# Weight conversion in a three-layer float32 kernel: two 512-column pieces at a time, in 1024-column instructions

## The chip, the cores and the metric

The kernel runs on one core of one Trainium2 chip. The metric is the device time of one execution in microseconds (us), lower is better. Before the change three runs gave 1316.76, 1318.71 and 1318.84 us; the median is 1318.71.

The engines are named as the profile names them: PE is TensorE's matmul unit and PEld its weight load, DVE is VectorE, ACT is ScalarE, POOL is GpSimd, SP is SyncE, whose queue issues the DMAs here.

## What is computed

Cut from the reference (B, H, S, Ns, D = 8, 8, 512, 32, 64; d_model 512, d_ff 2048):

```python
scores = scale * np.matmul(x, state.transpose(0, 1, 3, 2))
a = softmax(scores)                      # over the 32 states
xread = np.matmul(a, state)
a2 = softmax(scale * np.matmul(state, x.transpose(0, 1, 3, 2)))
sread = np.matmul(a2, x)
x = np.concatenate([xread, sread], axis=2)   # 8 x 544 rows of 512
x = square(relu(x @ w_in)) @ w_out       # the kernel's w1, v1
x = elu(x @ w_in2) @ w_out2              # the kernel's w2, v2
```

The four weight matrices arrive as float64 and everything else as float32. A float32 product is made of three PE passes: each operand is split into a high and a low part of the type float32r, and hi*lo, hi*hi and lo*hi are summed.

## The kernel before

**Stages.** The work on 8 batches of 544 rows has three parts. In the first, batches 0 to 3 go singly through attention and the first layer (16 steps of f, one for 128 of the 2048 hidden columns); batches 4 to 7 go in pairs by an algorithm of seven products. In the second part the rows of state go through the first layer. In the third the second layer runs, again by seven products. The change touches the weights, which are converted while batches 0 to 3 are worked on; three pairs of v2 follow with the last pair of batches.

**Weights.** A piece is 128 rows by 512 columns of float64, so 512 KB. `load64` (line 210) issues its load on SP as 1024 int32 a partition, into the next of RAW = 5 raw tiles of 4 KB. `convert` (line 218) makes float32 of it: on ACT a Prelu that scales the high words (line 228), then a copy that turns the low words into an integer part (line 230); on DVE a clamp (232), a shift by three bits (233), and the addition of the low part (235). Each of the five instructions is 512 columns wide.

**What the four kinds of piece become.** w1's 16 pieces go by twos into eight tiles that stay (`conv_w1`, line 237). v1's 16 pieces are stored to DRAM (`d_v`), and split at once into high and low part, on ACT (line 254) and on DVE (line 256) (`conv_v1`, line 247). w2 and v2 are made in pairs j and j + 8 by `conv_pair` (line 283), stored, and summed and split for the seven products (`wf`, `f_w`, `f_v`).

**The order.** The list `pieces` holds four pieces of w1, then v1 and w1 by turns. `next_conv` moves every conversion that is under way on by one step, and starts the next if the `cv` tiles (CV = 4, of 2 KB) allow it; it is called four times after the scores of batch 0, four times after the operand of batch 0, and twice in each of its steps f. `next_load` issues one more load once a piece's raw tile has been read. A scheduler in the framework then fixes the order of the instructions of each engine; buffers and order decide every wait. Engines take their queue in order, and so does SP.

**Batch 0 at the start.** The scores (`sc`, line 349) are made, then m = w1 x state for a quarter of the hidden columns (`emit_m`: `mp` in bursts of eight 32-column matmuls, copied by ACT, lines 362 and 364, with the matrix `minus` between them); four such quarters m_0 to m_3 serve the 16 steps. A step f makes `h` from m (6 matmuls, lines 170 to 172), then on ACT `r` = relu (487), `g` and `gs` = squares (489, 491), on DVE the low part of gs (492), and two steps later 12 matmuls into `acc` with v1's f. While PE would wait in the first 25 us, `busy_pe` (line 530) lets it multiply `ident` with itself (`idle`, line 534).

Of the kernel before, what the change touches and what calls it, by code (L numbers as in the profile page):

```python
# [11 lines left out]
I32 = mybir.dt.int32  # L12
# [15 lines left out]
LAG = 2  # L28
RAW, WF, CV = 5, 3, 4
NF = 7  # L30
# [80 lines left out]
def attn_mlp_kernel(ctx: ExitStack, tc: tile.TileContext, xt, xn, st, w1, v1, w2, v2, outx, outs):  # L111
# [46 lines left out]
    gap(pool, "gap3", 48)  # L158
    wo_p = pool("wo", FC)
    gs_p = pool("gs", 3)  # L160
# [20 lines left out]
    if True:  # L181
        ident = const.tile([P, P], F32, name="ident")
        make_identity(nc, ident)
        minus = const.tile([P, P], F32R, name="minus")
        nc.scalar.activation(out=minus, in_=ident, func=AF.Copy, scale=-1.0)
# [23 lines left out]

        def load64(name, i):  # L210

            t = turn("raw", [P, 512, 2], I32, f"raw_{name}{i}")
            nc.sync.dma_start(out=t.rearrange("p f w -> p (f w)"), in_=src64[name][i].bitcast(I32))
            raw[name, i] = t

        pace, gate = [], []

        def convert(name, i, out):

            t = raw.pop((name, i))
            low, high = t[:, :, 0], t[:, :, 1]
            bits = out.bitcast(I32)
            after = pace if name in ("w2", "v2") else gate
            with tc.issue_after(after[0].ins) if after else nullcontext():
                nc.scalar.activation(out=out, in_=high.bitcast(F32), func=AF.Prelu, scale=2.0 ** -112, alpha=NEGATIVE)
            with tc.issue_after(gate[0].ins) if gate else nullcontext():
                nc.scalar.activation(out=low, in_=low.bitcast(U32), func=AF.Copy, scale=2.0 ** -29)  # L230
            yield
            nc.vector.tensor_scalar(out=out, in0=out, scalar1=CLAMP, scalar2=-NEGATIVE * CLAMP, op0=ALU.min, op1=ALU.max)
            nc.vector.tensor_single_scalar(out=bits, in_=bits, scalar=3, op=ALU.logical_shift_left)
            yield
            nc.vector.tensor_tensor(out=bits, in0=bits, in1=low, op=ALU.add)
# [11 lines left out]
        def conv_v1(f):  # L247
            v = conv_p["cv"].tile([P, 512], F32, name="cv", tag="cv")
            yield from convert("v1", f, v)
            next_load()  # L250
            d = wd["v1", f] = dram.tile([P, 512], F32, name=f"d_v1{f}", tag=f"d_v1{f}")
            nc.sync.dma_start(out=d, in_=v)
            t = wo_p.tile([P, 2, DM], F32R, name=f"v1_{f}", tag="wo")
            nc.scalar.activation(out=t[:, HI], in_=v, func=AF.Copy)
            yield
            nc.vector.tensor_tensor(out=t[:, LO], in0=v, in1=t[:, HI].bitcast(F32), op=ALU.subtract)
            wo_t["v1", f] = t

# [24 lines left out]
        def conv_pair(name, j):  # L283


            v = [conv_p["cv"].tile([P, 512], F32, name="cv", tag="cv") for _ in range(2)]
            for _ in zip_longest(convert(name, j, v[0]), convert(name, j + HF, v[1])):
                yield
            next_load()
            next_load()  # L290
            d = wd[name, j] = dram.tile([P, 2, 512], F32, name=f"d_{name}{j}", tag=f"d_{name}{j}")
            for r in range(2):
                nc.sync.dma_start(out=d[:, r], in_=v[r])
            for t in sums(v):
                yield
            w = wf[name, j] = dram.tile([P, NF, 2, 256], F32, name=f"f_{name}{j}", tag=f"f_{name}{j}")
            yield from put_split(w, ((1, v[0][:, :256].unsqueeze(1)), (2, v[1].rearrange("p (q f) -> p q f", q=2)),
                                     (2, t[:, :2]), (2, t[:, 2:])))

        def sums_v1(j):  # L300

            v = [conv_p["cv"].tile([P, 512], F32, name="cv", tag="cv") for _ in range(2)]
            for r in range(2):
# [17 lines left out]
        of_pairs = lambda pairs: [(name, r * HF + j) for name, j in pairs for r in range(2)]  # L321
        loading, busy = pieces + of_pairs(pairs2[:IN_SINGLE]), []
        pairs2 = pairs2[IN_SINGLE:]

        def next_load():
            if loading:
                load64(*loading.pop(0))

        def next_conv(more=True):

            for c, name in list(busy):
                if next(c, busy) is not None:
                    busy.remove((c, name))
            held = sum({"w1": 0, "v1": 1}.get(n, 2) for _, n in busy)
            if more and converting and (converting[0][0] == "w1" or held + (converting[0][0] != "v1") < depth["cv"]):
# [87 lines left out]
        def at_sread(b):  # L423
# [103 lines left out]
        for _ in range(RAW):  # L527
            next_load()

# [10 lines left out]
        gate.append(A[0]["exp"])  # L540
        for _ in range(KC):
            next_conv()
# [4 lines left out]
        at_soft2(0)  # L547
        for _ in range(4):
            next_conv(False)
# [10 lines left out]
        gate.append(copies[0])  # L560
        for _ in range(4):
            next_conv()
        gate.clear()
        later = {}
        for b in range(SINGLE):
# [124 lines left out]
        converting.extend(pairs2)  # L690
        loading.extend(of_pairs(pairs2))
        for _ in range(2):
            next_load()
        products, left = iter(()), 0
# [398 lines left out]
```

## Time and profile before

| | |
|---|---|
| runs, median | 1318.71 us (1316.76 to 1318.84) |
| profiled execution, first to last instruction (span) | 1314.0 us |
| profiled execution, own time | among the runs' values, 2.8 to 4.8 us above its span |
| PE busy | 1302.9 us, 7020 matmuls on record |
| DVE busy | 952.7 us, 1431 instructions |
| ACT busy | 845.4 us, 1429 instructions |
| DMA | 305.40 MB, mean 232 GB/s |

The profile is one execution taken by the hardware profiler. A row of the order of time names the start, the duration, the engine, the line, the operation, the tiles written and read, their shape, and how many equal instructions were merged; in brackets stand the idle time of the engine ahead of it and what ended that. A float32 matmul with 32 columns counts as two, and some matmuls lack a record. The duration of an instruction overlaps with the next one's, so what an instruction takes of its engine is the distance from its start to the next start. One add of integers (line 235) is counted in 16-bit halves, so its 512 columns read as 1024.

### The profile page before, as it was taken

How to read it: one execution, taken by the hardware profiler on the slowest of the kernel's cores; microseconds unless marked ns; L12 is line 12 of the kernel's file. 1: busy time of each engine (PE TensorE's matmuls, PEld its weight loads, DVE VectorE, ACT ScalarE, POOL GpSimd, SP SyncE). 2: the span in 40 equal slices, each digit the busy share in tenths (PEclk: the TensorE clock that was granted, in tenths of full speed). 3: DMA queues.
4: the chain of work that ended last, by engine and by line, in shares of the span. 5: the costliest groups of instructions: out<-in, count | busy, mean ns of one | idle time of the engine just before them, and what ended most of it. 6: DMA issues, size and time to landing. Idle time of an engine off the chain costs nothing.

```text
span 1314.0 us, 19733 instructions
## 1 busy us (share of the span) xinstructions
PE 1302.9 (99%) x7020; PEld 1042.5 (79%) x7020; DVE 952.7 (73%) x1431; ACT 845.4 (64%) x1429; POOL 0.7 (0%) x6
## 2 busy tenths in 40 slices
PE   8999999999999999999999999999999999999999
PEld 6677777777677777778988888888888888888888
DVE  6997878687869955895766963789546984568644
ACT  5997777787765667665567744675446743666444
POOL 0000000000000000000000000000000000000000
PEclk9999999999999999999999999999999999999999
DMA  7999987886734663589697678767786777778733
GB/s 264 321 326 360 336 310 255 294 299 241 266 107 140 203 196 112 166 285 316 207 316 193 196 210 256 237 192 210 215 282 191 209 208 230 204 207 288 220 115 113
DMA packets 138865, 305.40 MB, mean 232 GB/s; under 512 B 14736, under 2 KB 29072, under 8 KB 135696
## 3 DMA queue, kind: packets, MB, share of 16 engines
q1 hardware_dynamic: 138768, 304.15, 72.0%
q8 instruction: 56, 0.92, 0.3%
q14 instruction: 41, 0.34, 0.1%
HBM read 227.54 MB, written 76.55 MB: 231 GB/s over the span
## 4 chain that ended last, share of the span: by engine, by line
PE 83%; DVE 5%; ACT 3%; DMA 3%; issue 1%; SPq 0%; ACTq 0%; DVEq 0%
PE x L44 18%; PE X L44 13%; PE z L44 9%; PE Z L44 6%; PE acc L170 4%; PE acc L172 4%; PE acc L171 4%; PE h L170 4%; PE h L172 4%; PE h L171 4%; PE y L44 3%; PE Y L44 3%; PE mp L349 2%; PE as L44 2%; PE hs L44 1%; DVE g L82 1%
## 5 line engine op out<-in xcount | busy, mean ns | idle before, releaser
L176 DVE TENSOR_TENSOR gp<-g,gp 128x512 fp32r<-128x512 f32 (+1 forms) x224 | 212.4, 955 | 110.9 <-ACT gp L175 109.9
L175 ACT ACTIVATE gp<-g 128x512 fp32r<-128x512 f32 (+1 forms) x224 | 187.4, 843 | 149.8 <-PE x L44 73.8
L44 PE MATMUL x<-gp,wr 128*128 128x512 f32 x1152 | 273.6, 391 | 1.2 <-DVE gp L176 1.1
L44 PEld LDWEIGHTS x<-gp,wr 128*128 128x128 f32 x1152 | 214.8, 188 | 52.9 <-DVE gp L176 4.1
L44 PE MATMUL X<-xf,wr 128*128 128x512 f32 x768 | 186.9, 390 | 0.1
L44 PEld LDWEIGHTS X<-xf,wr 128*128 128x128 f32 x768 | 143.4, 188 | 32.1 <-ACT u L879 1.7
L44 PE MATMUL z<-gp,wr 128*128 128x512 f32 x576 | 133.5, 390 | 0.0
L44 PEld LDWEIGHTS z<-gp,wr 128*128 128x128 f32 x576 | 108.0, 188 | 23.5 <-issue 0.8
L875 DVE SCALAR_TENSOR_TENSOR g<-r,g 128x512 f32<-128x512 f32 x96 | 63.9, 689 | 64.7 <-ACT r L874 64.6
L170 PE MATMUL acc<-gs,v 128*128 128x512 f32 x256 | 103.1, 403 | 0.1
L170 PE MATMUL h<-at,m 128*128 128x512 f32 x256 | 101.6, 397 | 0.8 <-ACT m L175 0.5
L172 PE MATMUL acc<-gs,v 128*128 128x512 f32 x256 | 100.3, 392 | 0.0
L171 PE MATMUL acc<-gs,v 128*128 128x512 f32 x256 | 100.0, 391 | 0.0
L171 PE MATMUL h<-at,m 128*128 128x512 f32 x256 | 99.9, 390 | 0.0
L172 PE MATMUL h<-at,m 128*128 128x512 f32 x256 | 99.9, 391 | 0.0
L44 PE MATMUL Z<-xf,wr 128*128 128x512 f32 x384 | 97.4, 389 | 0.0
L873 ACT ACTIVATE r<-g 128x512 f32<-128x512 f32 x96 | 57.5, 625 | 59.6 <-DVE g L923 42.8
L82 DVE TENSOR_TENSOR g<-g,g 128x1024 f32<-128x1024 f32 x72 | 87.5, 1221 | 0.7
L44 PEld LDWEIGHTS Z<-xf,wr 128*128 128x128 f32 x384 | 72.1, 188 | 15.0
L874 ACT ACTIVATE r<-r 128x512 f32<-128x512 f32 x136 | 81.5, 621 | 0.7
L170 PEld LDWEIGHTS acc<-gs,v 128*128 128x128 f32 x256 | 48.0, 188 | 26.6 <-issue 9.2
L44 PE MATMUL y<-gp,wr 128*128 128x512 f32 x288 | 68.6, 389 | 0.0
(148 smaller groups left out, 2039.4 us busy)
## 6 DMA issues: line engine op xcount, KB each, us to landing
wr<-f_v SPq DMA_DIRECT2D x288, 256.0 KB, 3.1
wr<-f_w SPq DMA_DIRECT2D x224, 256.0 KB, 3.0
f_v<-wf SPq DMA_DIRECT2D x40, 512.0 KB, 4.0
raw_w<-in_w_dram SPq DMA_DIRECT2D x32, 512.0 KB, 5.2
raw_v<-in_v_dram SPq DMA_DIRECT2D x32, 512.0 KB, 5.5
f_w<-wf SPq DMA_DIRECT2D x24, 512.0 KB, 3.7
wr<-p_v SPq DMA_DIRECT2D x48, 256.0 KB, 3.9
xt<-in_xt_dram SPq DMA_DIRECT2D x8, 1024.0 KB, 6.6
```

Source lines behind the costliest of these rows:

```text
L44: nc.tensor.matmul(ps, wk[a], xk[b], start=start and k == 0 and i == 0, stop=last and k == len(w) - 1 and i == 2, skip_group_check=True)
L82: return lambda jj: tt(out=out[jj], in0=a[jj], in1=b[jj], op=ALU.subtract)
L170: mm(ps, w[HI], x[LO], start=first, stop=False)
L171: mm(ps, w[HI], x[HI], start=False, stop=False)
L172: mm(ps, w[LO], x[HI], start=False, stop=last)
L175: copy = nc.scalar.activation(out=hi, in_=src, func=AF.Copy)
L176: nc.vector.tensor_tensor(out=lo, in0=src, in1=hi.bitcast(F32), op=ALU.subtract)
L349: mm(ps[e][32 * k:32 * k + 32, :], st_t[b][r, k, :], x(k, r), start=True, stop=True)
L873: act(out=r, in_=h, func=AF.Relu, scale=-1.0)
L874: act(out=r, in_=r, func=AF.Exp, scale=-1.0)
L875: nc.vector.scalar_tensor_tensor(out=out, in0=r, scalar=-1.0, in1=h, op0=ALU.add, op1=ALU.max)
```

## The change

Raw tiles hold two pieces (8 KB, three of them), each half filled by a load of its own (`load64` has the half, r, as an argument). A pair is pieces 2i and 2i + 1 for w1 and v1, and j and j + 8 for w2 and v2. `convert` is 1024 columns wide in all its five instructions, and the split of v1 too; v1 and the pairs are stored by one DMA each. Three raw tiles of two pieces take the place of five of one, and two `cv` tiles of 4 KB that of four of 2 KB; with batches 6 and 7 it is one of each. To make room `minus` is put into the tile of the sums (`tf`) and `srs` into that of the exponentials (`t`). `next_pair` issues two loads. `next_conv` is called half as often to start something, and as often to go on.

```diff
-RAW, WF, CV = 5, 3, 4
+RAW, WF, CV = 3, 3, 2
...
-    wo_p = pool("wo", FC)
+    wo_p = pool("wo", FC // 2)
...
-        minus = const.tile([P, P], F32R, name="minus")
+        minus = conv_p["tf"].tile([P, P], F32R, name="minus", tag="tf")
...
-        def load64(name, i):
-
-            t = turn("raw", [P, 512, 2], I32, f"raw_{name}{i}")
-            nc.sync.dma_start(out=t.rearrange("p f w -> p (f w)"), in_=src64[name][i].bitcast(I32))
-            raw[name, i] = t
+        def load64(name, i, r):
+
+            if r == 0:
+                raw[name, i] = turn("raw", [P, 2, 512, 2], I32, f"raw_{name}{i}")
+            n = i + r * HF if name in ("w2", "v2") else 2 * i + r
+            nc.sync.dma_start(out=raw[name, i][:, r].rearrange("p f w -> p (f w)"), in_=src64[name][n].bitcast(I32))
...
-            low, high = t[:, :, 0], t[:, :, 1]
+            low, high = t[..., 0], t[..., 1]
...
         def conv_w1(i):
-            g, k = divmod(i, KC)
-            if k % 2 == 0:
-                half[g, k // 2] = wi_p.tile([P, 2, 512], F32, name=f"w1_{g}{k // 2}", tag="wi")
-            t = half[g, k // 2]
-            yield from convert("w1", i, t[:, k % 2])
-            next_load()
-            if k % 2:
-                w1_t[g, k // 2] = t
...
+            t = wi_p.tile([P, 2, 512], F32, name=f"w1_{i}", tag="wi")
+            half[i // 2, i % 2] = t
+            yield from convert("w1", i, t)
+            next_pair()
+            w1_t[i // 2, i % 2] = t
...
+        def conv_v1(i):
+            v = conv_p["cv"].tile([P, 2, 512], F32, name="cv", tag="cv")
+            yield from convert("v1", i, v)
+            next_pair()
+            d = dram.tile([P, 2, 512], F32, name=f"d_v1{i}", tag=f"d_v1{i}")
             nc.sync.dma_start(out=d, in_=v)
...
+            t = wo_p.tile([P, 2, 2, DM], F32R, name=f"v1_{i}", tag="wo")
+            nc.scalar.activation(out=t[:, :, HI], in_=v, func=AF.Copy)
+            yield
+            nc.vector.tensor_tensor(out=t[:, :, LO], in0=v, in1=t[:, :, HI].bitcast(F32), op=ALU.subtract)
...
-            v = [conv_p["cv"].tile([P, 512], F32, name="cv", tag="cv") for _ in range(2)]
-            for _ in zip_longest(convert(name, j, v[0]), convert(name, j + HF, v[1])):
-                yield
-            next_load()
-            next_load()
+            v = conv_p["cv"].tile([P, 2, 512], F32, name="cv", tag="cv")
+            yield from convert(name, j, v)
+            next_pair()
...
-            for r in range(2):
-                nc.sync.dma_start(out=d[:, r], in_=v[r])
+            nc.sync.dma_start(out=d, in_=v)
+            v = (v[:, 0], v[:, 1])
...
-        pieces = [("w1", i) for i in range(4)]
-        for i in range(16):
-            pieces += [("v1", i)] + ([("w1", i + 4)] if i < 12 else [])
+        pieces = [("w1", i) for i in range(2)]
+        for i in range(8):
+            pieces += [("v1", i)] + ([("w1", i + 2)] if i < 6 else [])
...
-            sr = sm_p.tile([P, 2, D], F32, name=f"srs{b}", tag="srs")
+            sr = at_p.tile([P, 2, D], F32, name=f"srs{b}", tag="t")
...
                     at(i, next_conv)
-                    at(i, next_conv)
+                    at(i, next_conv, False)
...
-        depth.update(raw=2, wf=1, cv=2)
-        conv_p.update(raw=pool("raw2", 1), cv=pool("cv2", 2), tf=pool("tf2", 1))
+        depth.update(raw=1, wf=1, cv=1)
+        conv_p.update(cv=pool("cv2", 1), tf=pool("tf2", 1))
```

The first place is ACT's queue after the operand of batch 0 is copied (`at`), up to the squares of step 0; `cv` is v1's piece, `w_10` and `w_2` are the w1 tile of quarter 1's first half. Before:

```order
L228 ACTIVATE cv<-raw_v_167 128x512
L230 ACTIVATE raw_v_167<-raw_v_167 128x512
L228 ACTIVATE w_10_335<-raw_w_222 128x512
L230 ACTIVATE raw_w_222<-raw_w_222 128x512
L228 ACTIVATE cv<-raw_v_230 128x512
L230 ACTIVATE raw_v_230<-raw_v_230 128x512
L254 ACTIVATE v_0_343<-cv 128x512
L228 ACTIVATE w_10_335<-raw_w_278 128x512
L230 ACTIVATE raw_w_278<-raw_w_278 128x512
L487 ACTIVATE r<-h 128x512
```

And with the change:

```order
L228 ACTIVATE cv<-raw_v_165 128x1024
L230 ACTIVATE raw_v_165<-raw_v_165 128x1024
L228 ACTIVATE w_2_322<-raw_w_263 128x1024
L230 ACTIVATE raw_w_263<-raw_w_263 128x1024
L485 ACTIVATE r<-h 128x512
L251 ACTIVATE v_0_345<-cv 128x2x512
L487 ACTIVATE g<-r 128x512
L489 ACTIVATE gs<-r 128x512
```

The copy of v_0 has moved behind r, and r stands behind four conversions instead of eight and a copy.

The second place is PE's queue where the second half of m_3 is made (`mp_3` from `w_31`, the last w1 tile). Before:

```order
L349 MATMUL mp_3_1_1020<-w_31_857,st_155 32x512
L171 MATMUL acc<-gs,v_9_844 128x512
L172 MATMUL acc<-gs,v_9_844 128x512
L170 MATMUL acc<-gs,v_9_844 128x512
L171 MATMUL acc<-gs,v_9_844 128x512
L172 MATMUL acc<-gs,v_9_844 128x512
L170 MATMUL acc<-gs,v_9_844 128x512
L171 MATMUL acc<-gs,v_9_844 128x512
L172 MATMUL acc<-gs,v_9_844 128x512
L170 MATMUL acc<-gs,v_9_844 128x512
L349 MATMUL mp_3_0_1019<-w_31_857,st_155 32x512
L349 MATMUL mp_3_1_1020<-w_31_857,st_155 32x512
```

And with the change:

```order
L347 MATMUL mp_3_0_884<-w_6_690,st_155 32x512
L347 MATMUL mp_3_1_885<-w_6_690,st_155 32x512
L347 MATMUL mp_3_0_884<-w_6_690,st_155 32x512
L347 MATMUL mp_3_1_885<-w_6_690,st_155 32x512
L347 MATMUL mp_3_0_884<-w_7_788,st_155 32x512
L347 MATMUL mp_3_1_885<-w_7_788,st_155 32x512
L347 MATMUL mp_3_0_884<-w_7_788,st_155 32x512
L347 MATMUL mp_3_1_885<-w_7_788,st_155 32x512
L169 MATMUL acc<-gs,v_4_688 128x512
```

The eight are one burst now, where nine matmuls of acc stood between the sixth and the seventh.

The third place is PE's queue at the scores of batch 1 (`sc`). Before they were eight in a row; with the change:

```order
L170 MATMUL h<-at_312,m_11_514 128x512
L347 MATMUL sc_0_597<-xt_454,st_452 32x512
L171 MATMUL h<-at_312,m_11_514 128x512 x2
L347 MATMUL sc_1_598<-xt_454,st_452 32x512
L347 MATMUL sc_0_597<-xt_454,st_452 32x512
L347 MATMUL sc_1_598<-xt_454,st_452 32x512
L347 MATMUL sc_0_597<-xt_454,st_452 32x512
L347 MATMUL sc_1_598<-xt_454,st_452 32x512
L347 MATMUL sc_0_597<-xt_454,st_452 32x512
L347 MATMUL sc_1_598<-xt_454,st_452 32x512
L171 MATMUL acc<-gs,v_1_379 128x512
```

Two matmuls of h, which want the low part of m_11, have moved between the first of the scores and the other seven.

## Rows read from the trace of the kernel before

**Rows 1.** The page's first part: span, then busy time of each engine.

```profile
span 1314.0 us, 19733 instructions
...
PE 1302.9 (99%) x7020; PEld 1042.5 (79%) x7020; DVE 952.7 (73%) x1431; ACT 845.4 (64%) x1429; POOL 0.7 (0%) x6
```

**Rows 2.** Busy time by stretches: length, each engine, granted clock, DMA share, GB/s.

```profile
core 0: us, PE busy (x) PEld busy (x) DVE busy (x) ACT busy (x) POOL busy (x), PEclk, DMA share, GB/s
...
40.00:60.00 20.00, 19.91 (x96) 14.05 (x96) 18.23 (x39) 20.00 (x40) 0.00 (x0) 1.00 0.92 329
...
100.00:150.00 50.00, 49.64 (x262) 37.70 (x268) 40.24 (x78) 34.55 (x65) 0.00 (x0) 1.00 0.98 365
150.00:300.00 150.00, 150.00 (x902) 113.84 (x887) 119.16 (x242) 115.66 (x219) 0.00 (x0) 1.00 0.81 288
```

**Rows 3.** Order of time on PE around the scores of batch 1.

```profile
51.82 0.39 PE L171 MATMUL h<-at,m 128*128 128x512 f32 x1
52.05 0.39 PE L172 MATMUL h<-at,m 128*128 128x512 f32 x1
52.36 1.09 PE L349 MATMUL sc<-xt,st 64*32 64x512 f32 x16
...
53.72 0.39 PE L171 MATMUL acc<-gs,v 128*128 128x512 f32 x1
```

**Rows 4.** The same view around the products for m_2.

```profile
59.88 0.39 PE L171 MATMUL acc<-gs,v 128*128 128x512 f32 x1
60.75 1.67 PE L349 MATMUL mp<-w,st 64*32 64x512 f32 x12 [0.48 <-DVE t L384]
...
63.62 0.50 PE L172 MATMUL acc<-gs,v 128*128 128x512 f32 x1
```

**Rows 5.** The same view: the first h and the first acc.

```profile
26.76 0.50 PE L170 MATMUL h<-at,m 128*128 128x512 f32 x1
...
34.56 0.50 PE L170 MATMUL acc<-gs,v 128*128 128x512 f32 x1
```

**Rows 6.** Order of time on ACT, from 12 to 68 us.

```profile
12.24 0.67 ACT L228 ACTIVATE w<-raw_w 128x512 f32<-128x512 f32 x1
12.80 0.69 ACT L230 ACTIVATE raw_w<-raw_w 128x512 int32<-128x512 uint32 x1
...
26.01 0.67 ACT L228 ACTIVATE cv<-raw_v 128x512 f32<-128x512 f32 x1
...
31.06 0.57 ACT L487 ACTIVATE r<-h 128x512 f32<-128x512 f32 x1
...
32.09 0.61 ACT L489 ACTIVATE g<-r 128x512 f32<-128x512 f32 x1
32.61 0.62 ACT L491 ACTIVATE gs<-r 128x512 fp32r<-128x512 f32 x1
...
66.39 1.10 ACT L394 ACTIVATE t<-t 128x1024 f32<-128x1024 f32 x1
67.34 0.67 ACT L254 ACTIVATE v<-cv 128x512 fp32r<-128x512 f32 x1
```

**Rows 7.** Order of time on DVE, from 17 to 22 us.

```profile
17.33 1.22 DVE L393 TENSOR_TENSOR t<-t,m 128x1024 f32<-128x1024 f32 x1
18.46 0.69 DVE L235 CUSTOM_DVE_ANT_0 w<-raw_w,w 128x1024 uint16<-128x1024 uint16 x1
19.06 0.42 DVE L232 TENSOR_SCALAR w<-w 128x512 f32<-128x512 f32 x1
19.40 0.16 DVE L432 TENSOR_SCALAR z<-z 128x2 f32<-128x2 f32 x1
...
20.99 0.68 DVE L235 CUSTOM_DVE_ANT_0 w<-raw_w,w 128x1024 uint16<-128x1024 uint16 x1
```

**Rows 8.** A raw load's issue on SP, its first reading on ACT; median time to landing.

```profile
29.17 0.33 SPq L213 DMA_DIRECT2D raw_w<-in_w_dram  x1
...
34.22 0.65 ACT L228 ACTIVATE w<-raw_w 128x512 f32<-128x512 f32 x1
...
raw_w<-in_w_dram SPq DMA_DIRECT2D x32, 512.0 KB, 5.2
```

More of the change, by code (lines that the diff above doesn't have):

```diff
@@ L1 @@
 from contextlib import ExitStack, nullcontext
-from itertools import zip_longest
 import concourse.bass as bass
@@ L237, in conv_w1 @@
         def conv_w1(i):
-            g, k = divmod(i, KC)
-            if k % 2 == 0:
-                half[g, k // 2] = wi_p.tile([P, 2, 512], F32, name=f"w1_{g}{k // 2}", tag="wi")
-            t = half[g, k // 2]
-            yield from convert("w1", i, t[:, k % 2])
-            next_load()
-            if k % 2:
-                w1_t[g, k // 2] = t
-        def conv_v1(f):
-            v = conv_p["cv"].tile([P, 512], F32, name="cv", tag="cv")
-            yield from convert("v1", f, v)
-            next_load()
-            d = wd["v1", f] = dram.tile([P, 512], F32, name=f"d_v1{f}", tag=f"d_v1{f}")
+            t = wi_p.tile([P, 2, 512], F32, name=f"w1_{i}", tag="wi")
[8 more added lines that the diff above has]
+            d = dram.tile([P, 2, 512], F32, name=f"d_v1{i}", tag=f"d_v1{i}")
             nc.sync.dma_start(out=d, in_=v)
-            t = wo_p.tile([P, 2, DM], F32R, name=f"v1_{f}", tag="wo")
-            nc.scalar.activation(out=t[:, HI], in_=v, func=AF.Copy)
+            t = wo_p.tile([P, 2, 2, DM], F32R, name=f"v1_{i}", tag="wo")
+            nc.scalar.activation(out=t[:, :, HI], in_=v, func=AF.Copy)
             yield
-            nc.vector.tensor_tensor(out=t[:, LO], in0=v, in1=t[:, HI].bitcast(F32), op=ALU.subtract)
-            wo_t["v1", f] = t
+            nc.vector.tensor_tensor(out=t[:, :, LO], in0=v, in1=t[:, :, HI].bitcast(F32), op=ALU.subtract)
+            for r in range(2):
+                wd["v1", 2 * i + r], wo_t["v1", 2 * i + r] = d[:, r], t[:, r]
         wd, wf = {}, {}
@@ L283, in conv_pair @@
         def conv_pair(name, j):
-            v = [conv_p["cv"].tile([P, 512], F32, name="cv", tag="cv") for _ in range(2)]
-            for _ in zip_longest(convert(name, j, v[0]), convert(name, j + HF, v[1])):
-                yield
-            next_load()
-            next_load()
+            v = conv_p["cv"].tile([P, 2, 512], F32, name="cv", tag="cv")
+            yield from convert(name, j, v)
+            next_pair()
             d = wd[name, j] = dram.tile([P, 2, 512], F32, name=f"d_{name}{j}", tag=f"d_{name}{j}")
-            for r in range(2):
-                nc.sync.dma_start(out=d[:, r], in_=v[r])
+            nc.sync.dma_start(out=d, in_=v)
+            v = (v[:, 0], v[:, 1])
             for t in sums(v):
@@ L300, in sums_v1 @@
         def sums_v1(j):
-            v = [conv_p["cv"].tile([P, 512], F32, name="cv", tag="cv") for _ in range(2)]
+            v = conv_p["cv"].tile([P, 2, 512], F32, name="cv", tag="cv")
+            v = (v[:, 0], v[:, 1])
             for r in range(2):
@@ L315, in attn_mlp_kernel, with next_pair @@
         wo_t = {}
-        pieces = [("w1", i) for i in range(4)]
-        for i in range(16):
-            pieces += [("v1", i)] + ([("w1", i + 4)] if i < 12 else [])
+        pieces = [("w1", i) for i in range(2)]
+        for i in range(8):
+            pieces += [("v1", i)] + ([("w1", i + 2)] if i < 6 else [])
         pairs2 = [(name, j) for name in ("w2", "v2") for j in range(HF)]
         converting = pieces + [("f1", j) for j in range(HF)] + pairs2[:IN_SINGLE]
-        of_pairs = lambda pairs: [(name, r * HF + j) for name, j in pairs for r in range(2)]
-        loading, busy = pieces + of_pairs(pairs2[:IN_SINGLE]), []
+        of_units = lambda units: [(name, i, r) for name, i in units for r in range(2)]
+        loading, busy = of_units(pieces + pairs2[:IN_SINGLE]), []
         pairs2 = pairs2[IN_SINGLE:]
-        def next_load():
-            if loading:
-                load64(*loading.pop(0))
+        def next_pair():
+            for _ in range(2):
+                if loading:
+                    load64(*loading.pop(0))
         def next_conv(more=True):
@@ L333, in next_conv @@
                     busy.remove((c, name))
-            held = sum({"w1": 0, "v1": 1}.get(n, 2) for _, n in busy)
-            if more and converting and (converting[0][0] == "w1" or held + (converting[0][0] != "v1") < depth["cv"]):
+            held = sum(n != "w1" for _, n in busy)
+            if more and converting and (converting[0][0] == "w1" or held < depth["cv"]):
                 name, i = converting.pop(0)
@@ L527, in attn_mlp_kernel @@
         for _ in range(RAW):
-            next_load()
+            next_pair()
         def busy_pe(n):
@@ L540, in attn_mlp_kernel @@
         gate.append(A[0]["exp"])
-        for _ in range(KC):
+        for _ in range(2):
             next_conv()
@@ L547, in attn_mlp_kernel @@
         at_soft2(0)
-        for _ in range(4):
+        for _ in range(2):
             next_conv(False)
@@ L560, in attn_mlp_kernel @@
         gate.append(copies[0])
-        for _ in range(4):
+        for _ in range(2):
             next_conv()
@@ L690, in attn_mlp_kernel @@
         converting.extend(pairs2)
-        loading.extend(of_pairs(pairs2))
-        for _ in range(2):
-            next_load()
+        loading.extend(of_units(pairs2))
+        next_pair()
         products, left = iter(()), 0
```

## The prediction

> **What bounds the kernel now.** I read the page's first part, then the busy time by stretches, then the order of time on TensorE (PE), ScalarE (ACT) and VectorE (DVE) at the start. PE is busy for 1302.9 of 1314.0 us [rows 1]; the reader is to see that this leaves some 11 us of idle time in all, most of it before 40 us. From 150 to 300 us PE is busy for every one of 150 us; in the stretch from 100 to 150 it lacks 0.36 us [rows 2]. A change to conversions there can only lose. Before 100 us it is different: from 40 to 60 ACT is busy for 20.00 of 20 us and DVE for 18.23 [rows 2], and PE, nearly full, is fed by both.
>
> A busy PE is not PE at its peak, so I take prices from start to start. A 128x512 matmul follows the last after 0.23 us (51.82 to 52.05) [rows 3]. A burst of the small 32-column matmuls (scores, or the products for m) costs 1.2 us whatever its size up to 8: from 52.05 to 53.72 are 1.67 us, in which two big matmuls would have taken 0.45 [rows 3]. A burst that comes before its inputs costs more: m_2's stands between 59.88 and 63.62, 3.74 us, so 2.3 more than the 1.44 (1.67 less a matmul) that a ready one takes between such points [rows 4]. The first real matmul, h, starts at 26.76 and the first acc at 34.56 [rows 5].
>
> **The change, by prices.** Two conversions become one of twice the width. On ACT a 512-wide conversion comes every 0.56 us (12.24 to 12.80), and a 1024-wide activation is followed after 0.95 (66.39 to 67.34), while a 512-wide square takes 0.52 (32.09 to 32.61) [rows 6]. So 512 more columns cost 0.43, and a 1024-wide conversion 0.56 + 0.43 = 0.99, if what it takes over a square is fixed, or 0.95 x 0.56 / 0.52 = 1.03, if it goes by the column. A merged pair saves 0.13, or 0.09; I take 0.13, since the trace has only 512-wide rows of that kind and both ends are near. [...]
>
> On DVE the clamp and the shift come every 0.34 us at 512 (19.06 to 19.40), the add every 0.60 (18.46 to 19.06), and a 1024-wide subtraction is followed after 1.13 (17.33 to 18.46) [rows 7]. So a merged clamp costs 0.60, a merged add or subtraction 1.13: each merge saves 0.07. In all 72 ACT, 104 DVE and 24 DMA instructions go and none is added. That is 8 to 9 us of ACT and 7 of DVE, but all behind 100 us lies beside a full PE and counts for nothing; what counts is the 8 v1 and 8 w1 pairs of the start, 32 conversions and 8 copies on ACT: 0.13 x 32 + 0.09 x 8 = 4.9 us.
>
> **The first 27 us: -0.2.** DVE works without a gap up to the last w1 add, begun at 20.99 [rows 7]. The four pieces cost 8 x 0.335 + 4 x 0.60 = 5.1 there, and as two pairs 4 x 0.60 + 2 x 1.13 = 4.7; two small z instructions now stand ahead of it (0.2). The last add ends 0.2 earlier, and m, atf and the first h with it: 26.76 becomes 26.6.
>
> **To the first acc: -1.3.** Before, ACT begins the next conversions at 26.01 and reaches r, which frees the h bank, at 31.06, behind eight conversions and one copy [rows 6]. The order of the change puts only four wide conversions ahead of r: 25.8 + 4 x 0.99 = 29.8. Behind r stand the wide copy of v_0 (0.95), g and gs (0.95 + 3 x 0.5 with r), so gs ends at about 32.4 and its DVE half 0.7 later; acc starts at 33.2 or 33.3 instead of 34.56 [rows 5]. With 1.03 a conversion it is 33.5 and the term -1.1.
>
> **From there to 97 us: -0.8.** I follow the changed order with the same prices. The conversions gained on PE: m_2's burst is broken by waits of 2.3 us, and m_3's comes in two bursts, one too many (1.2), with 0.25 of a gap for v_3; 3.75 to be had. Taken back: the scores of batch 1 now come as one matmul, a pair of h, and seven, so one burst more, 1.2. m_2 still waits, since DVE does the v_3 subtraction (1.13) and the w_5 add (1.13) and the gs subtractions ahead of the transposes that free its banks: PE is there at 59.2, the transposes end at 59.7: 0.5, and 0.2 before it for gs of f = 4. m_3's second half needs w_7's add, which by the chain on DVE ends at 80.0 with PE there at about 79: 1.0 with the wait for m_2's copy, which stands in ACT behind v_4's. Sum of these 2.9; net -0.8. Work on PE is otherwise the same (6388 instructions in both), and its order after 100 us too, so what is won there stays. **Sum: -0.2 is inside the -1.3; -1.3 - 0.8 = -2.1.** With none of the waits it is -1.3 - 3.75 + 1.2 = -3.9; with 1.03 a conversion ACT falls 28 x 0.04 = 1.1 us behind, and it is -1.0.
>
> **Loads.** Each queue entry counts: SP now issues two raw loads at once when a tile is free, and one 512 KB store where there were two of 256. A raw load issued at 29.17 was first read at 34.22 [rows 8]; such loads take 5.2 us in the median [rows 8], so there was next to nothing to spare. Of the change, w_3's two halves go out at 29.9 (v_0's add ends there) and are read at 35.8, so the later half has 5.4 us; later tiles by the same walk have 1 to 4 us more. Three tiles of two hold six pieces where there were five. I cost it at nothing: its cover is those 0.2 to 4 us, and if it is gone each load that is late stops ACT, and r behind it.
>
> The tiles that moved cost nothing: minus is last read before the first tf of the v1 sums, and the new home of srs is read by PE before the next scores are made, so each is covered by an order that exists.
>
> The sum is made against the profiled execution, whose span is 1314.0; 2.8 to 4.8 us lie around it in the runs shown, 4.7 at their median of 1318.7. **1318.7 - 2.1 = 1316.6 us.**
>
> **Rivals.** (A) The waits that I add don't come, since DVE and ACT are both shorter by more than I count, and the whole -3.9 stays: 1314.8. For it: ACT was full from 40 to 60 [rows 2] and gains 4.9. Against it: DVE has 18.23 of 20 there and gains less, 56 merges of 0.07, which are 3.9 us up to 97. (B) The gain goes into loads: second halves land late in the start, and ACT gives back what it won. It needs only three late loads of 0.6 us each, ahead of an r that PE waits for; against it, the DMA engines are used at 0.92 from 40 to 60, and reach 0.98 from 100 to 150 [rows 2], so there is some room. Then 1318.4. [...]
>
> **Numbers.** The forecast has 0.50, with 1315.2 to 1318.1 as its own range; A 0.22, B 0.17, C 0.11. About 0.2% (2.6 us, below 1316.1) is what a measurement of this kernel can tell. A third of the forecast and all of A lie below it: 0.39. Above 1321.3 lies most of C, and I add a little for late loads that stop PE outright: 0.12. The rest, 0.49, is within. The range runs from the -3.9 and a little beyond, 1314.0, to the half of C's price, 1320.4.
>
> **What would show it.** Right: wide conversions at 0.97 to 1.05 from start to start; r at about 29.8; the first acc at 33.2 to 33.6; one burst each for m_2 and m_3, and two for the scores of batch 1; PE the same after 112 us but 2 us earlier. Wrong: idle time of ACT ahead of a conversion for a raw load before 90 us (B); a granted clock under 1.00 between 20 and 40 us (C); m_3's burst before 78 us (A); or PE gaps after 112 us, which nothing here foresees.

## The result, and the profile after

The changed kernel takes 1327.18 us in the median (1323.96 to 1328.66, six runs), the kernel before 1317.03 (1315.41 to 1318.84, six runs). The ratio is 1.0071 with an interval of 1.0060 to 1.0082: some 9 us slower. The forecast was 1316.6 with a range up to 1320.4, so it is wrong, and outside its range.

The profiled execution of the change has a span of 1326.9 us, 12.9 over that of before. A run takes 1.8 us more than its span, so the two took some 1328.7 and 1315.8 us, one of the slowest of the change and one of the fastest of before (not 2.8 to 4.8 us over its span, as I had put it): with medians 10 apart, this pair shows the loss at nearly its largest. Its first page answers to [rows 1]:

```profile
span 1326.9 us, 19507 instructions
...
PE 1305.3 (98%) x7020; PEld 1045.1 (79%) x7020; DVE 946.2 (71%) x1327; ACT 840.5 (63%) x1357; POOL 0.7 (0%) x6
```

ACT and DVE have less to do, as the change says, and PE is busy 2.4 us longer for the same 7020 instructions. The stretches of [rows 2], with two more behind them (length, busy time of each engine, granted clock, DMA share, GB/s):

```profile
100.00:150.00 50.00, 46.63 (x230) 35.14 (x229) 34.80 (x68) 30.02 (x56) 0.00 (x0) 0.93 0.93 340
150.00:300.00 150.00, 149.89 (x888) 113.98 (x888) 116.56 (x208) 110.53 (x193) 0.00 (x0) 1.00 0.80 287
300.00:350.00 50.00, 47.49 (x310) 34.31 (x309) 38.14 (x69) 34.18 (x62) 0.00 (x0) 1.00 0.73 266
350.00:400.00 50.00, 47.47 (x327) 32.83 (x326) 32.79 (x56) 34.52 (x62) 0.00 (x0) 0.97 0.44 147
```

Before, the last two of these read:

```profile
300.00:350.00 50.00, 49.50 (x322) 35.91 (x321) 42.47 (x82) 36.80 (x71) 0.00 (x0) 1.00 0.80 278
350.00:400.00 50.00, 50.00 (x343) 35.38 (x342) 31.72 (x53) 34.47 (x61) 0.00 (x0) 1.00 0.37 119
```

From 150 to 300 us next to nothing is lost. The loss sits in 100 to 150 us, where PE now lacks 3.4 us instead of 0.4 and the granted clock falls, and in 300 to 400, where it lacks 5 us instead of 0.5. That can be counted without windows. Both kernels have 4904 matmuls of 128x512, and from the 301st on PE takes them in the same order. Their start times (us) in the traces of the two kernels and of three runs told below:

| start of the | first scores | 1st | 25th | 301st | 351st | 1001st | 1301st | 4801st |
|---|---|---|---|---|---|---|---|---|
| before | 8.27 | 23.45 | 35.59 | 114.40 | 127.02 | 293.01 | 379.56 | 1242.58 |
| change | 7.56 | 22.54 | 34.37 | 113.97 | 132.71 | 299.12 | 392.20 | 1255.48 |
| low words last | 7.56 | 22.54 | 34.38 | 113.36 | 130.07 | 296.82 | 384.58 | 1246.38 |
| copies on ScalarE | 8.17 | 23.15 | 36.10 | 114.90 | 127.51 | 293.93 | 384.35 | 1247.14 |
| both | 7.53 | 22.51 | 34.34 | 113.44 | 126.06 | 293.49 | 381.55 | 1241.94 |

Part of the lead at the start is luck. 40 filler matmuls stand ahead of the first scores in every one of these kernels; they come every 0.21 us at first and then every 0.11, and the moment of that change of pace differs from execution to execution, here 6.1 us in the trace of before and 4.6 in that of the change (the granted clock is on record only from that moment on, at 1.00). PE's rows:

```profile
1.35 6.99 PE L534 MATMUL idle<-ident 128*128 128x128 f32 x40 [1.35 <-POOL ident masks.py:199]
...
1.35 6.28 PE L532 MATMUL idle<-ident 128*128 128x128 f32 x40 [1.35 <-POOL ident masks.py:199]
```

The first row is of before, the second of the change. So the scores begin 0.71 us earlier with the change, and two more traces with the start of before have them at 7.52 and 8.78. Counted from the scores the change is 0.2 us ahead at the first matmul, 0.5 at the 25th and 0.3 behind at the 301st. Then it loses 6.1 us in fifty matmuls (18.7 us against 12.6) and 6.5 more between the 1001st and the 1301st (93.1 against 86.6). Behind that next to nothing moves.

**The first place.** PE, in order of time (start, duration, what ended the wait):

```profile
118.30 0.39 PE L171 MATMUL acc<-gs,v 128*128 128x512 f32 x1
122.05 0.80 PE L169 MATMUL acc<-gs,v 128*128 128x512 f32 x1 [3.37 <-DVE oo L518]
122.65 0.63 PE L170 MATMUL acc<-gs,v 128*128 128x512 f32 x1
123.07 0.63 PE L171 MATMUL acc<-gs,v 128*128 128x512 f32 x1
...
126.91 0.63 PE L171 MATMUL h<-at,m 128*128 128x512 f32 x1
```

Batch 1's first accumulation waits until DVE has copied batch 0's accumulators out of their banks. Instead of 0.23 us the next matmul comes after 3.75, so 3.5 are lost; and what follows comes every 0.43 us, up to 127, at a granted clock of 0.50: from 122.05 to 126.91 are eleven steps in 4.86 us, against 2.50 at the 0.227 us a step of a clock of 1.00, so another 2.4. Together 5.9 of the 6.1. What held DVE:

```profile
111.38 0.69 DVE L490 TENSOR_TENSOR gs<-g,gs 128x512 fp32r<-128x512 f32 x1 [0.35 <-ACT gs L489]
117.87 0.42 DVE L263 TENSOR_TENSOR tf<-cv 128x256 f32<-128x256 f32 x1 [5.80 <-DMA cv<-d_v]
...
119.70 0.43 DVE L264 TENSOR_TENSOR tf<-cv 128x256 f32<-128x256 f32 x1 [0.20 <-DMA cv<-d_v]
...
121.31 0.68 DVE L518 COPY oo<-acc 128x512 f32<-128x512 f32 x1
```

The first of v1's sums (L263) stands in DVE's queue ahead of the copy (L518), and waits 5.8 us for v1 to come back from DRAM. In the kernel before, the sums of the same pair stand ahead of the copy too, but their reload lands 5.5 us earlier. The copy begins at 117.62, PE's next three matmuls of acc begin at 118.28 without a wait, and nothing is to spare:

```profile
112.74 0.42 DVE L265 TENSOR_TENSOR tf<-cv 128x256 f32<-128x256 f32 x1
114.20 0.43 DVE L266 TENSOR_TENSOR tf<-cv 128x256 f32<-128x256 f32 x1 [1.05 <-DMA cv<-d_v]
...
117.62 0.69 DVE L520 COPY oo<-acc 128x512 f32<-128x512 f32 x1
```

SP of the change shows why it lands late (start and duration of issues):

```profile
92.77 1.07 SPq L214 DMA_DIRECT2D raw_w<-in_w_dram  x2
93.89 0.42 SPq L249 DMA_DIRECT2D d_v<-cv  x1
95.38 1.26 SPq L302 DMA_DIRECT2D cv<-d_v  x2
...
105.69 0.32 SPq L278 DMA_DIRECT2D f_v<-wf  x1
...
106.58 0.73 SPq L194 DMA_DIRECT2D xt<-in_xt_dram  x1
...
107.91 0.43 SPq L302 DMA_DIRECT2D cv<-d_v  x1
```

SP stands before the raw load at 92.77 until a whole pair is converted (5.9 us of waiting for the add of line 235). The last v1 piece goes out behind it as one 512 KB store at 93.89; the sums follow late, the store of their first result (105.69) has moved ahead of batch 2's x in the queue, and the third pair's reload is issued at 107.91 behind 1 MB of x. It lands at 117.78 by the trace, 9.9 us later. Before, x went out at 101.22, the reload at 104.63, and landed at 112.30.

**The second place.** PE's waits, 100 to 360 us (total, times, longest):

```profile
PE acc L169 <- DVE oo L518: 3.4, 1, 3.4
PE h L169 <- ACT m L174: 2.5, 1, 2.5
PE tp L417 <- DVE m L175: 1.5, 1, 1.5
PE sc L347 <- DVE stf L442: 1.0, 1, 1.0
```

Before, the same view has two waits of 0.5 and 0.4, although ACT waits there for raw loads of v2 too (7.5 us in five between 245 and 335 us, the longest 3.4; with the change 10.0 in four). The waits for tp (at 308) and sc (at 337) follow on waits of ACT for raw loads of v2, the one for h (at 352) on a wait of ACT for a `wf` tile that is still being stored:

```profile
256.00 1.13 ACT L230 ACTIVATE raw_v<-raw_v 128x1024 int32<-128x1024 uint32 x1 [3.09 <-DMA raw_v<-in_v_dram]
...
300.13 1.11 ACT L230 ACTIVATE raw_v<-raw_v 128x1024 int32<-128x1024 uint32 x1 [2.83 <-DMA raw_v<-in_v_dram]
...
330.35 1.13 ACT L230 ACTIVATE raw_v<-raw_v 128x1024 int32<-128x1024 uint32 x1 [2.29 <-DMA raw_v<-in_v_dram]
...
353.73 0.63 ACT L276 ACTIVATE wf<-tf 128x512 fp32r<-128x512 f32 x1 [1.91 <-DMA f_v<-wf]
```

The low words (L230) need no `cv` tile, so the scheduler puts them right behind the reload of a raw tile, long before the high words of the same pair. A raw tile is now reloaded only when both its halves are converted, with 1 MB at once, and ACT is there 2 to 3 us too soon. Whatever else feeds PE queues behind: the splits of the sums, which DVE waits for in turn with the splits of m (tp) and the copies of the transposes (sc) behind them, and their stores, which are then late for the next splits (h).

### The profile page after: what moved, and what is told of

Read it like the earlier page. It is cut to its first block, busy times and chain, and to the rows that moved or that the text cites. A ratio compares the mean times of both kernels' runs of the same rounds, so it can differ in the third digit from the quotient of the medians.

```text
span 1326.9 us, 19507 instructions
## 1 busy us (share of the span) xinstructions
PE 1305.3 (98%) x7020; PEld 1045.1 (79%) x7020; DVE 946.2 (71%) x1327; ACT 840.5 (63%) x1357; POOL 0.7 (0%) x6
## 4 chain that ended last, share of the span: by engine, by line
PE 85%; DVE 8%; DMA 3%; ACT 2%; issue 2%; SPq 0%; POOLq 0%; ACTq 0%; DVEq 0%; POOL 0%
PE x L43 19%; PE X L43 13%; PE z L43 10%; PE Z L43 7%; PE y L43 4%; PE h L169 4%; PE h L171 4%; PE h L170 4%; PE acc L169 3%; PE Y L43 3%; PE acc L171 3%; PE acc L170 3%; DMA raw_v<-in_v_dram 2%; PE mp L347 2%; PE as L43 2%
## 5 line engine op out<-in xcount | busy, mean ns | idle before, releaser
L169 PEld LDWEIGHTS acc<-gs,v 128*128 128x128 f32 x256 | 48.3, 188 | 32.8 <-issue 12.6
```

What stands on the lines that cost most here:

```text
L169: mm(ps, w[HI], x[LO], start=first, stop=False)
```

## The experiments

**Undo the width: all, the late half, the early half.** The five instructions of `convert` are cut into two of 512 columns; tiles, loads and stores stay as in the change. `parts` is `[slice(0, 1), slice(1, 2)]`, or `[slice(0, 2)]` where the width stays.

```diff
-                nc.scalar.activation(out=out, in_=high.bitcast(F32), func=AF.Prelu, scale=2.0 ** -112, alpha=NEGATIVE)
+            for s in parts:
+                nc.scalar.activation(out=out[:, s], in_=high[:, s].bitcast(F32), func=AF.Prelu, scale=2.0 ** -112, alpha=NEGATIVE)
...
```

> Every conversion instruction of the changed kernel cut back to 512 columns, tiles and loads as in the change. If the width of the instructions is what costs (an in-order engine held 0.5 us longer at a time), the time comes back to 1317 +- 2 us. If the pairing of tiles and loads costs (a tile is reloaded only when both its halves are converted, and the sums of v1 reload late), the wait of TensorE for accumulators near 120 us stays at 3 to 4 us and the time stays between 1322 and 1329 us, with ScalarE's waits for raw loads shorter than the 3.1, 1.8, 2.8 and 2.3 us of the change because a half needs only its own load.

> Only the conversions of w2 and v2 cut back to 512 columns, w1 and v1 stay 1024 wide. If a wide read waits for the later of two loads and so holds ScalarE (theory: late half), TensorE's waits between 300 and 400 us (1.65 for tp, 1.6 for sc, 2.9 for h) shrink below 1 us each and the time falls by 3 to 6 us to 1321 to 1324; the wait of 3.7 us near 120 us stays. If the late half is not the cause: 1325 to 1329 us with the same three waits.

> The mirror of the second run: the conversions of w1 and v1 cut back to 512 columns, those of w2 and v2 1024 wide, tiles and loads as in the change. With 1327.2 (both wide), 1329.5 (late ones halved) and 1323.7 (both halved) it completes a square. If the width of w1 and v1 alone decides whether the copy near 118 us is late, that wait is under 1 us here and the waits of 300 to 355 us stay as in the change: 1321 to 1324 us, and the first 512-column matmul starts near 26 us instead of 23. If the pairing of tiles decides both: 1326 to 1331 us.

| w1, v1 | w2, v2 | median | ratio to before, interval |
|---|---|---|---|
| 1024 | 1024 (the change) | 1327.18 | 1.0071, 1.0060 to 1.0082 |
| 1024 | 512 | 1329.53 | 1.0089, 1.0068 to 1.0110 |
| 512 | 1024 | 1327.61 | 1.0073, 1.0059 to 1.0086 |
| 512 | 512 | 1323.72 | 1.0047, 1.0029 to 1.0065 |

All four are slower than before, but not all for the same reasons. From the 1001st to the 1301st matmul they take 93.1, 93.3, 92.3 and 91.5 us, in the order of the table, where the kernel before takes 86.6: for the second place tiles and loads by twos are enough, whatever the width. The first place wants wide conversions of w1 and v1 as well: the fifty matmuls from the 301st take 18.7 and 14.2 us with these, and 12.6 and 12.9 without. There DVE waits 0.6 us for the reload, and PE is 1.6 and 3.1 us later at the 301st than in the change. So the wait near 120 us does not stay with all widths halved, as the first of these expectations had it for the case that pairing costs, though its time fell into the range given for that. What this kernel loses besides lies at the start (below).

The theory of the late half falls: with the late conversions cut, ACT's waits for raw loads of v2 grow from 10.0 us in four to 14.0 in seven (245 to 335 us), and the wait of the scores near 337 us from 1.0 to 3.3. The lateness is of the load as a whole. The expectation for the early half alone missed in part: its copy is in time, as the first way wanted, but the first matmul comes at 24.07, not near 26, the second place costs what it cost, and the time is in the range of the second way.

**Cure the second place: low words last.**

```diff
-                nc.scalar.activation(out=out, in_=high.bitcast(F32), func=AF.Prelu, scale=2.0 ** -112, alpha=NEGATIVE)
-            with tc.issue_after(gate[0].ins) if gate else nullcontext():
+                first = nc.scalar.activation(out=out, in_=high.bitcast(F32), func=AF.Prelu, scale=2.0 ** -112, alpha=NEGATIVE)
+            with tc.issue_after((gate or [first])[0].ins) if gate or name in ("w2", "v2") else nullcontext():
```

> One line: in w2 and v2 the low words are scaled after the high words' conversion (the change has them first, as soon as the raw tile has landed), all instructions 1024 wide. Theory late half: by the time a cv tile is free the loads have landed, ScalarE's waits for raw loads of v2 between 245 and 335 us (10 us in four) fall under 3 us, the three waits of TensorE between 300 and 400 us go, time 1321 to 1324 us. If the width itself costs: no change, 1325 to 1329 us. A third way: the conversion ends later, so the next loads go out later and the waits only move, same time or slower.

1320.64 us (1317.57 to 1323.86, ten runs), ratio 1.0019 (1.0005 to 1.0033). ACT's waits, 245 to 335 us, no longer hold a raw load:

```profile
ACT r L485 <- PE h L171: 18.8, 12, 3.2
ACT wf L276 <- DMA f_v<-wf: 1.4, 1, 1.4
ACT e L380 <- DVE mx L379: 1.2, 2, 1.0
ACT wf L276 <- DVE tf L267: 0.7, 1, 0.7
```

The stretch from the 1001st to the 1301st matmul takes 87.8 us instead of 93.1. Of PE's three waits there the scores' is gone and the others are 0.8 and 1.3 us. The instructions are as wide as in the change, so neither their width nor the later half is the cause here, but where the scheduler put the reading. The line does more than it was meant to: it also moves ACT's order from 92 us on and DVE's from 98 on, and the fifty matmuls of the first place take 16.7 us in this trace instead of 18.7, so not all of the 6.5 us that it gains are the second place's.

**Cure the first place: copies on ScalarE.**

```diff
-                if k % 2:
+                if k % 2 and b:
                     nc.vector.tensor_copy(out=o, in_=acc[k])
```

> One line: the two copies of batch 0's accumulators that VectorE makes go to ScalarE; nothing else moves. Theory: VectorE stands 5.8 us before the sums of v1 for a reload that lands at 117.8 us, its copy behind that is late, and TensorE waits 3.7 us for the bank and then runs some 5 us at the lower clock. Then the wait shrinks under 1 us, the clock of 115 to 130 us goes from 0.77 to 1.00, and the time falls by 4 to 7 us to 1320 to 1323 us. Rival: the second operand half (gs, also VectorE) is as late as the copy, TensorE waits for that instead, and the time stays between 1326 and 1329 us.

1323.23 us (1320.65 to 1326.23, seven runs), at the upper edge of what was expected; ratio 1.0047 (1.0031 to 1.0063). DVE still waits 4.8 us for the reload, and PE no longer for DVE; the row of DVE, and the stretch from 115 to 130 us:

```profile
117.04 0.43 DVE L263 TENSOR_TENSOR tf<-cv 128x256 f32<-128x256 f32 x1 [4.82 <-DMA cv<-d_v]
```

```profile
115.00:130.00 15.00, 15.00 (x78) 11.45 (x77) 9.36 (x20) 8.57 (x18) 0.00 (x0) 1.00 1.04 408
```

In the change this stretch has 11.63 us of PE and a clock of 0.77 (the columns are those above):

```profile
115.00:130.00 15.00, 11.63 (x52) 7.93 (x51) 8.05 (x16) 5.34 (x10) 0.00 (x0) 0.77 1.02 394
```

The fifty matmuls take 12.6 us, as before the change. So the fall of the clock near 120 us went with the wait: without the wait the granted clock is 1.00 in this stretch.

**Both cures, and the same cures on the kernel before.**

> The edits of the runs before put together: batch 0's copies all on ScalarE, and the low words of w2 and v2 scaled last; every instruction, tile and load of the change is as wide as in the change. Theory two causes (VectorE's reload wait near 112 us and ScalarE's raw waits between 245 and 335 us): the gains add, 4.0 + 6.5 us off 1327.2, so 1315 to 1319 us, and the trace has no TensorE wait over 1.5 us behind 100 us and no stretch at the lower clock. If a third cost of the change's own is left: 1320 to 1323 us.

> The kernel before with the same one line (low words of w2 and v2 scaled last). Theory: its raw waits (0.8 to 1.8 us, one of 3.4) cost TensorE under 1 us, since no wait of it behind 120 us is over 0.9 us; so no change, 1315.5 to 1319.5 us, ratio 0.998 to 1.002. Rival: the line is good in itself and repairs nothing that the change brought; then 1311 to 1314 us.

> The kernel before with the copies of batch 0 on ScalarE: the control for that repair. In it VectorE's copies stand ahead of the sums that wait for the reload, and TensorE has no wait over 0.9 us near 118 us, so no change: ratio 0.998 to 1.002. If the repair is good in itself: 1312 to 1315 us.

Both on the change: 1318.16 us (eleven runs), ratio 1.0003 (0.9994 to 1.0012). The whole loss is gone with every instruction as wide and every load as large as in the change. On the kernel before the low words last give 1316.06 us, 0.9993 (0.9983 to 1.0003), and the copies 1316.43, 0.9997 (0.9988 to 1.0007). The cures are worth nothing where there is nothing to cure. (In the last expectation the order is put too simply: in the kernel before the copies stand behind the sums of the third pair and ahead of those of the fourth.) One part of the expectation missed: near 302 and 344 us PE stands 1.3 and 1.8 us from start to start in the cured kernel, of which the view counts 1.0 and 1.4 as idle,

```profile
PE h L169 <- ACT m L174: 1.4, 1, 1.4
PE tp L417 <- DVE m L175: 1.0, 1, 1.0
PE acc L169 <- ACT oo L520: 0.5, 1, 0.5
```

and the kernel before has the first two as well with the same line (1.4 and 1.0 us), so they come with that cure. (The profiled execution of that control is the slowest of its eleven, 1320.49; its median shows no price.)

**Is it the place in SyncE's queue?**

```diff
-                at(12 if b else 13, load_x, nb + 1)
+                at(12 if b else 14, load_x, nb + 1)
```

> The changed kernel with one number changed: the load of batch 2's x is called one step later (14 for 13), which puts it behind the third pair of reloads for the sums of v1 in SyncE's queue. Theory: the reload lands at 117.8 us, 9.9 us after its issue, because 1 MB of x stands ahead of it; then it lands 3 to 4 us earlier, VectorE's wait falls from 5.8 to 1 to 3 us, TensorE's wait of 3.7 us under 1.5 us, and the time is 1321 to 1324 us. Rival: the slot for it comes free late and the other stores fill the queue; it lands no earlier than 116 us, and the time is 1326 to 1329 us.

> All three edits on the changed kernel. If the copies and the place of x cure the same wait, the time is that of the two edits alone, within 1.5 us; if the late x also delays other work (VectorE's sums, the second operand half), 1 to 3 us less than that, 1313 to 1316 us, which would be under the kernel before.

Alone: 1324.30 us, 0.3 over the range, 1.0047 (1.0031 to 1.0064). The reload is issued at 107.39, lands at 113.40 instead of 117.78, DVE waits 2.37 us, and no matmul behind 100 us runs at the lower clock (0.43 us a step). PE waits 1.5 us, now for ACT's copy, as expected at the upper end. With the two cures it gains nothing more: 1319.60, 1.0018 (1.0008 to 1.0029), which is 1.4 us over these alone, within the 1.5 expected, and the intervals overlap. The trace has a loss, though, 16.7 us for the fifty matmuls. The sums moved one place in ACT's queue, to the front of the copies that had been moved there to be out of their way:

```profile
116.11 0.63 ACT L276 ACTIVATE wf<-tf 128x512 fp32r<-128x512 f32 x1 [3.48 <-DVE tf L267]
...
118.64 1.08 ACT L520 ACTIVATE oo<-acc 128x512 f32<-128x512 f32 x2
```

It is the wait of the first place once more, on another engine.

**What is the width worth by itself?** Both cures, with all conversions cut to 512 columns.

> All conversions cut back to 512 columns, tiles and loads of the change, with the two one-line repairs (copies on ScalarE, low words of w2 and v2 last). Against 1318.2 us of the same repairs with wide instructions it prices the width by itself. If the 2.5 to 3 us that the wide instructions win before the first matmul stay won: 1320 to 1322 us. If the steps before 100 us absorb them, as the equal losses at 100 us of the two runs with halves say: 1317 to 1319.5 us.

1321.31 us, 1.0030 (1.0018 to 1.0041), against 1.0003 with wide instructions: about 3.5 us, as the first way had it. Where they come from is less simple. The first big matmul comes at 25.68 instead of 22.51, but 1.3 of these 3.2 us are the fillers again (scores at 8.82 and 7.53). Counted from the scores it comes after 16.86 us, 0.3 of which go with a stretch at the lower clock (the first two big matmuls take 1.28 us there, and 0.98 with both cures and wide instructions), and with the early conversions alone halved, at the full clock, after 16.59; wide it takes 14.98, and the kernel before 15.18. So pairing the tiles costs 1.4 us at the start and the width brings back 1.6. The rest of the 3.5 lies in the second place, where the halved kernel takes 90.9 us and the wide one 88.1.

**Out of SyncE's way.** On top of both cures:

```diff
-                nc.sync.dma_start(out=w[:, first:first + n], in_=h.bitcast(F32))
+                nc.gpsimd.dma_start(out=w[:, first:first + n], in_=h.bitcast(F32))
```

> The change with both repairs, and the 512 KB stores of split weights (f_v, f_w) issued from POOL's queue instead of SyncE's. In the change SyncE stands 58.7 us of 225 to 345 us before these stores for VectorE, with the raw loads and reloads queued behind. Theory: with the stores out of the way the loads go out when their slots come free, the remaining TensorE waits of the repaired kernel (1.3 us near 302, 1.8 us near 344) shrink under 1 us, 1313 to 1316 us, under the kernel before. Rival: the loads are bound by their slots, not by the queue, no change against 1318.2 us (1316.5 to 1320). Third: issue from POOL is dear or holds VectorE, and the time is over 1321 us, with VectorE's mean instruction longer.

1337.12 us, 1.0140 (1.0120 to 1.0160): the worst of all, and by the mechanism of none of the three ways. PE's waits from 100 to 400 us, and ACT's longest but for those on PE:

```profile
PE acc L169 <- ACT oo L520: 5.7, 1, 5.7
PE h L169 <- ACT o L520: 3.3, 1, 3.3
PE tp L417 <- DVE m L175: 2.4, 1, 2.4
```

```profile
ACT wf L276 <- DMA f_v<-wf: 19.1, 8, 7.6
```

The 512 KB stores of f_v land later (5.1 us in the median instead of 4.1; those of f_w do not, 4.3 against 4.4), and ACT stands 7.6 us before one of the three `wf` tiles with the copies behind it. Another 8 us are lost behind the 1301st matmul (868.6 us to the 4801st, against 860.4 with the stores on SP), which I did not follow. DVE is busy 947.3 us, against 945.7 with the stores on SP, so it isn't held by POOL.

## Why the prediction was wrong

**The prices held.** On ACT a 1024-wide conversion takes 1.04 us from start to start (median), where I took 0.99 and had 1.03 as the other end; a pair of 512 takes 1.13, so a merge saves 0.09: the other end was nearer than my choice of 0.13. On DVE the merged clamp has 0.61 and the add 1.14, as forecast.

**The start held in part, and its number by luck.** r comes at 29.23 (forecast 29.8) and the first acc at 33.34 (33.2 or 33.3) instead of 34.56 [rows 5]. But 0.7 of that are the fillers, which ended earlier in this trace. Counted from the scores r gains the 1.1 us of its four conversions, and acc only 0.5 instead of 1.3. The step that my walk left out: PE's burst for the next quarter stands ahead of acc and waits for DVE's add, 0.25 us before and 0.88 with the change:

```profile
33.59 1.04 PE L349 MATMUL mp<-w,st 64*32 64x512 f32 x2 [0.25 <-DVE w L235]
...
32.39 1.02 PE L347 MATMUL mp<-w,st 64*32 64x512 f32 x2 [0.88 <-DVE w L235]
```

m_2 and m_3 come in one burst each, at 60.71 and 81.03, and the scores of batch 1 in two. One reading was wrong: of some 11 us that PE is idle in the kernel before, only 4.35 lie ahead of 40 us, not most.

**"From there to 97 us: -0.8" was of the wrong sign.** From the 25th matmul to the 301st the change takes 79.6 us, 0.8 more than before; the other traces with the same start have 78.8 to 80.5, those of before 78.8 to 79.0. Two waits that my walk lacks are most of the 0.8: acc for a late gs,

```profile
56.17 0.50 PE L169 MATMUL acc<-gs,v 128*128 128x512 f32 x1 [0.86 <-DVE gs L490]
...
89.89 0.50 PE L361 MATMUL mp<-m,minus 128*128 128x512 f32 x1 [0.56 <-ACT m L360]
```

and m_3's second step for its copy on ACT. The first is in all eight traces with this start, the second in three (0.4 to 1.0 us).

**The step that failed:** "all behind 100 us lies beside a full PE and counts for nothing", with its twin, that PE's "order after 100 us too" is the same, "so what is won there stays". PE's order was the same; the orders of DVE, ACT and SP were not, and each of the two losses comes from one of these: 6.1 us at 118, where DVE waits 5.8 us for a reload that SP issued late, with the copy behind it, and 6.5 us between 293 and 392, where ACT stands 10.0 us before raw loads. I had read from PE 49.64 of 50 us busy [rows 2] that conversions there could only lose, and then gave the loss no price. The trace of before had one to give: a DMA share of 0.98 in that stretch [rows 2], a reload under way for 7.7 us (issued 104.63, landed 112.30), DVE in order behind it, and a copy with nothing to spare. The gaps of PE behind 112 us are the last of my signs of being wrong, the one "which nothing here foresees".

**"Loads: I cost it at nothing"** was right for the start, where ACT waits 1.3 us for raw loads up to 110 us in all. One of these waits, 0.9 us at 85, is the sign of rival B, which wanted three of 0.6; its 1318.4 would still have been near no change. But I walked the loads only as far as the start. The same doubt, tiles reloaded by twos and ACT in order behind them, cost most of the 6.5 us of PE between 293 and 392 us (5.3 come back with the low words last).

**Rival C** was that PE's clock falls near the start, where PE has gaps. No run shows its price, half of which is in the range's upper end of 1320.4; it was my estimate, and the runs showed the following in its place. In the trace of the change the granted clock is 1.00 from 20 to 100 us; it fell to 0.50 at the two longest waits, 3.75 us at 118 and 2.92 at 352, for eleven and five steps of a matmul (0.43 us each instead of 0.23). The fall adds 2.4 us to a wait of 3.5 at the first, so this wait of PE cost more than its length. But the start of the change is in eight traces, and in four of them the clock fell there, as in that of the copies on ScalarE, whose orders on all engines are the change's up to 115 us (columns as above, granted clock 0.91):

```profile
20.00:40.00 20.00, 15.21 (x120) 9.37 (x120) 16.94 (x26) 16.24 (x22) 0.00 (x0) 0.91 0.81 282
```

From 18 to 22 us PE is busy for 1.8 to 2.0 of 4 us in all eight, and for 4.0 in the three traces with the start of before, none of which has a fall. Counted from the scores, the 25th matmul then comes 1.1 to 1.4 us later than at the full clock, and 0.6 to 0.9 later than before: C's sign, at that price.

The cause is shown as far as both cures and both controls go: two places, of 6.1 and 6.5 us, account for the change's whole loss. That x ahead of it makes the reload late is shown by the one number that moves x (4.4 of the 5.5 us). Which of the paired tiles, raw or `cv`, moved SP's order was not tried separately, and of the wide conversions, which the first place needs as well, the runs show no more than that with them halved DVE waits less for the reload and PE comes later.

## What to carry to other kernels

When conversions or loads are made twice as large, compare the order of every in-order queue, not that of the bottleneck engine alone, and look in each for an instruction that waits on a DMA with a bank release behind it. Larger tiles came free later and all at once here, and a reader that the scheduler had put right behind the reload waited with everything that was queued after it (ACT stood 10.0 us in four waits). Instruction overhead saved early is worth what it says only if no later wait is lengthened, and here two edits of a line or two, to the place of work, gave back 9 us, where the width of the instructions earned 3.5. And before a fraction of a microsecond at the start is put down to a change, count from a point that both kernels reach alike: the two traces here differed by 0.7 us before any changed instruction had run.

## What the runs showed of the hardware

After the wait of 3.75 us PE took eleven steps in 4.86 us, at a granted clock of 0.50 from the first (0.50 from 120.68 to 127.51); after the one of 2.92 us five steps took 1.32 us at a clock of 1.00 (354.90 to 356.22), and then five came every 0.43 us at 0.50. A shorter one was followed by this pace as well: with the early conversions halved, a wait of 1.5 us before the scores at 334.83, and then five matmuls every 0.43 us. In the run that moves x, one of 1.5 us near 119 was followed by none. The 40 fillers at the start, the same in every kernel, ended at 7.63 us in one trace and 8.34 in another: their pace went from one every 0.21 us to one every 0.11 earlier in the one (at 4.6 us) than in the other (at 6.1). The 512 KB stores of f_v landed 1 us later in the median when POOL issued them instead of SP (5.1 against 4.1 us), and ACT's longest wait for its tile grew to 7.6 us.
